# Operands stacked to 128 rows or columns in a recurrent-attention stage, and the powers and sums of its triangular inverse formed together

## The chip, the cores and the metric

One core of one Trainium2 chip runs the whole program. The metric is the device time of one launch in microseconds (us). Work is spread over TensorE (PE; its weight loads are shown apart as PEld), VectorE (DVE), ScalarE (ACT), GpSimd (POOL), and the DMA queue of SyncE (SP).

## What is computed

Two blocks follow each other: a recurrent attention (4 sequences, 8 heads, 768 tokens, head size 40), whose output rows then go through a mixture of 8 experts.

```python
for t in range(S):                       # state: 40x40 per sequence and head
    y[:, :, t] = einsum('bhd,bhde->bhe', r_t, state)
    Sa = einsum('bhde,bhe->bhd', state, a_t)
    state = state * w_t[:, :, None, :] - einsum('bhd,bhe->bhde', Sa, b_t)
    state = state + einsum('bhd,bhe->bhde', v_t, k_t)
x = y rearranged to (3072, 320)
expert = argmax(x @ w_gate); p = softmax weight of that expert
out = p * (relu(x @ w1[expert]) @ w2[expert])
```

## The kernel before

**Units.** The attention is cut into chunks of C = 64 tokens. One unit is one chunk of two sequences with all their heads (16 heads, laid out as NP = 4 pairs by two halves of the 128 partitions, each half holding 40 rows of a head). There are 24 units (12 chunks, two pairs of sequences in turn); a unit needs the state that the unit two before it left. Every product is in f32, and a matmul in f32 shows as two matmul records and two weight-load records in the trace; a transpose shows as one of each.

**What a unit does** (`unit`, L363 to L683). SP loads the decay (`dec`, L387) and one tile `in` with the five operands k, a, b, v, r (L388): four DMAs each. DVE scans the decay into running products (L389, L397), and POOL scales b, a and k by them (L400). Then PE works in steps, and each step's result in PSUM is taken out by DVE or ACT:

- `p_n` (L428): the products of a and b in both orders, 32 matmuls; masked by DVE (L436) they give the strictly triangular matrix N and its transpose, both in `X`.
- The inverse of the triangular matrix, as a product of (1 + N^k) for k = 1, 2, 4, ..., 32 (L440 to L494). `plus_one` on POOL adds the identity (L442); `moved` carries the transposed factor to the other halves (L463, four matmuls with 256 moving columns); `squares` (L474) squares both N^k and its transpose, 32 matmuls, four times, and a last `times` squares one of them, 16 matmuls; `times` (L445) multiplies each new factor on, 16 matmuls, five times, and `new_TT` copies the product out.
- `p_g` (L500): k with a and v with r, 32 matmuls, masked into `G` (L508). `natural` (L405): transposes of v, k and b, four each.
- The recurrent part: `p_r` (L528, 16 matmuls), `p_gv` (L535, 32), `p_u` (L557, 32), `p_uT` (L581, 16), `p_st` (L593, 32: the new state), `p_z` (L615, 16), `p_y` (L625, 32 in two steps), and `p_x` (L647, four matmuls with 128 stationary and 136 moving columns) that turns the output and forms the expert logits. The last part (L642 to L683) stores the rows of x.

Nearly all of these matmuls have 64 contraction rows and 64 stationary columns, and the loops go round `TILES` (L272), the four quarters of the 128x128 array.

**What sets the order.** Nothing runs as written. Every piece is a `Step` (L181) with a rank, an engine, a cost in us and its readers and writers; `in_order` (L201) picks, again and again, the step that can begin first by these costs (then the lowest rank), finds it PSUM banks (8 in all, two for most steps), and issues it. A step marked ANY goes to ACT or DVE, whichever is free first (L236). The order on each engine is fixed by that list; the engines wait for each other by semaphores. A `Ring` (L281) is a set of buffers taken in turn.

**Expert weights.** `w_pool` (L156) holds two sets of weights. `first_weights` (L688) loads the sets of experts 0 and 1 in the middle of the attention; later sets are loaded two experts ahead (L871). After the attention come routing (L696 to L798), then for each expert gather, transposes, layer 1 (L821), layer 2 (L836) and the scattered store.

Of the kernel before, what the change touches and what calls it, by code (L numbers as in the profile page):

```python
# [23 lines left out]
def kernel(  # L24
# [62 lines left out]

    ihalf = consts.tile([128, HP], F32)
    m_nn = consts.tile([128, 2, C], F32)
    m_up = consts.tile([128, C], F32)  # L90
    nc.gpsimd.memset(m_nn[:], -1.0)
    nc.gpsimd.memset(m_up[:], 1.0)
    for h in range(2):
        hs = slice(h * HP, (h + 1) * HP)
        nc.gpsimd.tensor_copy(ihalf[hs], ident[hs, hs])
        nc.gpsimd.affine_select(
            m_nn[hs, 0, :], m_nn[hs, 0, :], compare_op=ALU.is_gt, fill=0.0, base=0, pattern=[[-1, C]], channel_multiplier=1,
        )
        nc.gpsimd.affine_select(
            m_nn[hs, 1, :], m_nn[hs, 1, :], compare_op=ALU.is_gt, fill=0.0, base=0, pattern=[[1, C]], channel_multiplier=-1,  # L100
        )
        nc.gpsimd.affine_select(
            m_up[hs], m_up[hs], compare_op=ALU.is_gt, fill=0.0, base=0, pattern=[[1, C]], channel_multiplier=-1,
        )
# [51 lines left out]
    w_pool = ctx.enter_context(tc.tile_pool(name="moe_w", bufs=2))  # L156

    def fetch(w1, w2):
        t1 = w_pool.tile([128, DB, F], F32, name="w1")
        t2 = w_pool.tile([128, FB, Dm], F32, name="w2")  # L160
# [11 lines left out]
    PE, DVE, ACT, POOL, SP, ANY = "PE", "DVE", "ACT", "POOL", "SP", "ANY"  # L172
    steps = []
# [7 lines left out]
    class Step:  # L181
        def __init__(self, rank, eng, cost, fn, reads=(), writes=(), after=(), lag=0.2):
            self.rank, self.eng, self.cost, self.fn, self.lag = (rank, len(steps)), eng, cost, fn, lag
# [17 lines left out]
    def in_order():  # L201

        free = {e: 0.0 for e in (PE, DVE, ACT, POOL, SP)}
        bank_free = [0.0] * 8

# [25 lines left out]
        while ready:  # L231
# [26 lines left out]
            free[e] = t + cost  # L258
            s.done = t + cost + s.lag
# [16 lines left out]
    with tc.tile_pool(name="ring", bufs=1) as ring, \  # L276
# [18 lines left out]
        r_in = Ring("in", [5, SEG, C], 4, 5)  # L295
# [5 lines left out]
        r_nat = [Ring("nat" + n, [NP, 2, HP], 3) for n in "VKB"]  # L301
        r_X = Ring("X", [2, 2, NP, C], 5, 2)
        r_M = Ring("M", [2, NP, C], 3)
        r_TT = Ring("TT", [2, NP, C], 4)
        r_G = Ring("G", [2, 2, NP, C], 2, 2)
# [3 lines left out]
        r_U = Ring("U", [2, NP, D], 2)  # L309
        r_uT = Ring("uT", [2, NP, C], 2)  # L310
        r_ZT = Ring("ZT", [2, NP, C], 2)
# [10 lines left out]
        for i, (t, held) in enumerate(r_dec.bufs):  # L322
# [5 lines left out]
            Step(-100 + 5 * i, DVE, 1.2, fn, writes=held)  # L328
# [31 lines left out]
        eye = ihalf[:, None, None, :].to_broadcast([128, 2, NP, C])  # L360
        state = {}

        def unit(u):  # L363
            c, bh = divmod(u, BH)
            last = c + 1 == NCH
            I, hI = r_in.take()
            (dec, hdec), (qi, hqi), (rv, hrv), (qq, hq), (pc, hpc) = (r.take() for r in (r_dec, r_qini, r_rv, r_q, r_pc))
            r3 = rv[:, : SEG * C1].rearrange("p (s j) -> p s j", j=C1)
            q3 = qq[:].rearrange("p (s j) -> p s j", j=C1)
            behind = rv[:, 2:].rearrange("p (s j) -> p s j", j=C1)[:, :, :C]  # L370


            at, w0 = divmod(c * C, CW)
            dst = dec[:, : SEG * C1].rearrange("x (p q j) -> x q p j", q=2, j=C1)
            dst5 = I[:].rearrange("x n (p q) j -> x q n p j", q=2)

            def load(e, part):
                for q in range(2):
                    for par in range(2):
                        src = packed[2 * bh + q, at, par, :, :, :, w0 : w0 + C]  # L380
                        if part == 0:
                            nc.sync.dma_start(dst[rows(par), q, :, 1:], src[:, 0])
                        else:
                            nc.sync.dma_start(dst5[rows(par), q], src[:, 1:])
# [15 lines left out]
            for n, by, hb in ((B_, behind, hrv), (A, q3[:, :, :C], hq), (K, behind, hrv)):  # L400
                Step(pre, POOL, 1.22, lambda e, n=n, by=by: nc.gpsimd.tensor_tensor(I[:, n], I[:, n], by, op=ALU.mult),  # L401
                     reads=hb, writes=hI[n : n + 1])


            def natural(rank, r, n):  # L405
                t, hn = r.take()
                ps = Held(1)

                def turned(e):
                    for p in range(NP):  # L410
                        nc.tensor.transpose(  # L411
                            psum[:, ps.at, p * 128 : (p + 1) * 128], I[:, n, 2 * p : 2 * p + 2, :].rearrange("x q t -> x (q t)"),
                            ident[:],
                        )
                Step(rank, PE, 0.55, turned, reads=hI[n : n + 1], writes=[ps])
                Step(rank, ANY, 0.59, lambda e: copy(e, t[:].rearrange("c p a d -> c (p a d)"), psum[:, ps.at, :]),
                     reads=[ps], writes=hn)
                return t, hn

            def head(n, p, q, par):  # L420
                return I[halves[par], n, 2 * p + q, :]

# [5 lines left out]
            def p_n(e, ps=ps):  # L428
                t = whole(ps)
                for p in range(NP):  # L430
                    for w, (l, r) in enumerate(((A, B_), (B_, A))):
                        for par, q in TILES:
                            mm(t[halves[1 - q], par, w, p, :], head(l, p, q, par), head(r, p, q, par))
            Step(u, PE, 8 * ROUND, p_n, reads=[hI[A], hI[B_]], writes=[ps])
            for s in range(2):
                Step(u, DVE, 0.69, lambda e, s=s, ps=ps, X=X: nc.vector.tensor_tensor(  # L436
                    X[:, s], whole(ps)[:, s], m_nn[:, :, None, :].to_broadcast([128, 2, NP, C]), op=ALU.mult,
                ), reads=[ps], writes=hX[s : s + 1])

            def plus_one(x, hx, w):  # L440
                m, hm = r_M.take()
                Step(u, POOL, 1.25, lambda e: nc.gpsimd.tensor_tensor(m[:], x[:, :, w], eye, op=ALU.add), reads=hx, writes=hm)  # L442
                return m, hm

            def times(stat, mov, reads, ps):  # L445

                def fn(e):
                    t = pair(ps, C)
                    for p in range(NP):
                        for h, s in TILES:  # L450
                            mm(t[halves[s], h, p, :], stat(h, s, p), mov(h, s, p))
                Step(u, PE, 4 * ROUND, fn, reads=reads, writes=[ps])

            def new_TT(ps):
                t, ht = r_TT.take()
                Step(u, ANY, 0.59, lambda e: copy(e, t[:], pair(ps, C)), reads=[ps], writes=ht)
                return t, ht


            T1, hT1 = plus_one(X, hX, 1)  # L460
            ps = Held(2)

            def moved(e, ps=ps):  # L463
                t = pair(ps, C)
                for h, s in TILES:
                    mm(t[halves[s], h].rearrange("x p j -> x (p j)"), ihalf[halves[h]], T1[halves[h], s].rearrange("x p j -> x (p j)"))
            Step(u, PE, 4 * ROUND, moved, reads=hT1, writes=[ps])
            TT, hTT = new_TT(ps)
            k = 1
            while 2 * k < C:  # L470
                nk = 2 * k
                ps = Held(2)
                if 2 * nk < C:
                    def squares(e, ps=ps, X=X):  # L474
                        t = whole(ps)
                        for p in range(NP):
                            for w in range(2):
                                for h, s in TILES:
                                    mm(t[halves[s], h, w, p, :], X[halves[h], s, 1 - w, p, :], X[halves[h], s, w, p, :])
                    Step(u, PE, 8 * ROUND, squares, reads=hX, writes=[ps])  # L480
                    X, hX = r_X.take()
                    for s in range(2):
                        Step(u, ANY, 0.59, lambda e, s=s, ps=ps, X=X: copy(e, X[:, s], whole(ps)[:, s]),
                             reads=[ps], writes=hX[s : s + 1])
# [438 lines left out]
```

## Time and profile before

| | us |
|---|---|
| three runs | 1102.62, 1093.54, 1095.27 |
| median of the runs | 1095.27 |
| the profiled execution, its own time | 1102.44 |
| its span, from first to last instruction | 1100.7 |

The profile is of one execution. Its views used below: the page's totals; the waits (who waited for whom, in total us, times, longest); the timeline (instructions of one kind merged: start, length from the first start to the last end, engine, line, operation, tiles, shape, count, and in brackets the idle time before it and what ended it; "issue" means that the engine waited for nothing that the profile shows); the groups by line and shape (busy us, mean ns of one | idle time before); and tables of stretches. Lengths of matmul records overlap each other, so the pace of a run of them is read from one start to the next. The attention runs from about 30 to 719 us, the rest of the span is routing and the experts.

### The profile page before, as it was taken

How to read it: one execution, taken by the hardware profiler on the slowest of the kernel's cores; microseconds unless marked ns; L12 is line 12 of the kernel's file. 1: busy time of each engine (PE TensorE's matmuls, PEld its weight loads, DVE VectorE, ACT ScalarE, POOL GpSimd, SP SyncE). 2: the span in 40 equal slices, each digit the busy share in tenths (PEclk: the TensorE clock that was granted, in tenths of full speed). 3: DMA queues.
4: the chain of work that ended last, by engine and by line, in shares of the span. 5: the costliest groups of instructions: out<-in, count | busy, mean ns of one | idle time of the engine just before them, and what ended most of it. 6: DMA issues, size and time to landing. Idle time of an engine off the chain costs nothing. (4 is left out here: it accounts for less than half of the span.)

```text
span 1100.7 us, 50357 instructions
## 1 busy us (share of the span) xinstructions
PE 837.7 (76%) x23644; PEld 614.6 (56%) x23644; DVE 400.8 (36%) x769; ACT 247.5 (22%) x504; POOL 340.1 (31%) x318
## 2 busy tenths in 40 slices
PE   1676776876676667676777676728999999999996
PEld 1666666765665556666766665612535535535534
DVE  5445444454444434544554444361120110111110
ACT  1233333322223323223322232300101011010000
POOL 9544333343433413433343332125202202101001
PEclk9999899899989979998999899957999999999998
DMA  5222222222220381221222100003322223113000
GB/s 104 49 40 53 46 46 47 43 49 40 44 51 8 76 222 29 46 46 35 57 47 46 34 11 16 11 6 96 94 93 87 90 81 106 60 55 113 12 6 19
DMA packets 112678, 60.95 MB, mean 55 GB/s; under 512 B 96849, under 2 KB 108115, under 8 KB 112468
## 3 DMA queue, kind: packets, MB, share of 16 engines
q1 hardware_dynamic: 109056, 48.51, 19.0%
q0 software_dynamic: 3072, 9.18, 2.9%
q8 instruction: 186, 3.05, 1.2%
q14 instruction: 24, 0.20, 0.1%
q10 hardware_dynamic: 340, 0.01, 0.0%
HBM read 49.82 MB, written 9.18 MB: 54 GB/s over the span
## 5 line engine op out<-in xcount | busy, mean ns | idle before, releaser
L442 POOL TENSOR_TENSOR M<-X,ihalf 128x512 f32<-128x512 f32 x120 | 165.0, 1378 | 349.3 <-DVE X L355 194.0
L358 PE MATMUL ps<-X 64*64 64x64 f32 x6912 | 148.1, 228 | 68.3 <-issue 67.0
L827 PE MATMUL hp<-xgT,w 128*128 128x512 f32 (+1 forms) x384 | 192.2, 630 | 0.0
L358 PEld LDWEIGHTS ps<-X 64*64 64x64 f32 x6912 | 131.1, 142 | 79.2 <-issue 75.7
L840 PE MATMUL zp<-w,h_sb 128*128 128x320 f32 x512 | 145.0, 433 | 0.0
L827 PEld LDWEIGHTS hp<-xgT,w 128*128 128x128 f32 (+1 forms) x384 | 63.4, 190 | 123.4 <-issue 122.3
L358 PE MATMUL ps<-TT,M 64*64 64x64 f32 x3840 | 94.9, 228 | 37.2 <-issue 36.7
L353 ACT COPY TT<-ps 128x512 f32<-128x512 f32 x122 | 71.6, 587 | 193.5 <-PE ps L358 187.0
L840 PEld LDWEIGHTS zp<-w,h_sb 128*128 128x128 f32 x512 | 94.5, 191 | 34.5 <-issue 0.8
L832 DVE TENSOR_SCALAR h_sb<-hp 128x512 f32<-128x512 f32 x32 | 22.1, 692 | 247.5 <-PE hp L827 244.4
L358 PEld LDWEIGHTS ps<-TT,M 64*64 64x64 f32 x3840 | 79.5, 141 | 45.2 <-issue 43.2
L353 ACT COPY X<-ps 128x512 f32<-128x512 f32 x109 | 62.8, 587 | 172.0 <-PE ps L358 170.0
L355 DVE COPY X<-ps 128x512 f32<-128x512 f32 x83 | 57.3, 690 | 107.6 <-PE ps L358 106.2
L846 POOL DMA_INDIRECT out_dram<-zo,s_idx x32 | 31.7, 992 | 181.3 <-ACT zo L845 180.1
L358 PE MATMUL ps<-in 64*64 64x64 f32 x3072 | 61.6, 223 | 23.8 <-issue 23.5
L401 POOL TENSOR_TENSOR in<-in,rv 128x512 f32<-128x512 f32 x48 | 60.8, 1276 | 47.5 <-DMA in<-in_packed_dram 39.6
L411 PE MATMUL ps<-ident,in 128*128 128x128 f32 x288 | 48.8, 309 | 28.6 <-DMA in<-in_packed_dram 21.3
L358 PEld LDWEIGHTS ps<-in 64*64 64x64 f32 x3072 | 54.7, 137 | 27.2 <-issue 26.5
L834 ACT ACTIVATE h_sb<-hp 128x512 f32<-128x512 f32 x32 | 19.1, 597 | 203.1 <-PE hp L827 164.5
L808 POOL DMA_INDIRECT xg<-x_rows,g_idx x32 | 30.8, 963 | 109.0 <-PE tp L818 78.9
L411 PEld LDWEIGHTS ps<-ident,in 128*128 128x128 f32 x288 | 35.0, 155 | 34.0 <-issue 25.2
L845 ACT COPY zo<-zp 128x320 f32<-128x320 f32 x32 | 13.6, 426 | 134.3 <-PE zp L840 134.3
(163 smaller groups left out, 1072.5 us busy)
## 6 DMA issues: line engine op xcount, KB each, us to landing
in<-in_packed_dram SPq DMA_DIRECT2D x96, 200.0 KB
w<-in_moe_w_dram SPq DMA_DIRECT2D x8, 1280.0 KB
w<-in_moe_w_dram SPq DMA_DIRECT2D x8, 1024.0 KB
dec<-in_packed_dram SPq DMA_DIRECT2D x96, 40.0 KB
x_rows<-xs SPq DMA_DIRECT2D x48, 80.0 KB
w<-in_moe_w_dram SPq DMA_DIRECT2D x8, 256.0 KB
xg<-x_rows,g_idx POOLq DMA_INDIRECT x32
out_dram<-zo,s_idx POOLq DMA_INDIRECT x32
```

Source lines behind the costliest of these rows:

```text
L353: nc.scalar.copy(dst, src)
L355: nc.vector.tensor_copy(dst, src)
L358: nc.tensor.matmul(out_, lhsT=lhsT, rhs=rhs, start=start, stop=stop, skip_group_check=True)
L401: Step(pre, POOL, 1.22, lambda e, n=n, by=by: nc.gpsimd.tensor_tensor(I[:, n], I[:, n], by, op=ALU.mult), reads=hb, writes=hI[n : n + 1])
L411: nc.tensor.transpose(psum[:, ps.at, p * 128 : (p + 1) * 128], I[:, n, 2 * p : 2 * p + 2, :].rearrange("x q t -> x (q t)"), ident[:],)
L442: Step(u, POOL, 1.25, lambda e: nc.gpsimd.tensor_tensor(m[:], x[:, :, w], eye, op=ALU.add), reads=hx, writes=hm)
L808: nc.gpsimd.indirect_dma_start(out=g["xg"][:, j, :], out_offset=None, in_=x_d[:, :], in_offset=bass.IndirectOffsetOnAxis(ap=g["gi"](j), ax ...
L827: nc.tensor.matmul(hp[:, :cols], lhsT=g["w"][0][:dsz, db, fb * 128 : (fb + 1) * 128], rhs=g["xT"][:dsz, db, :cols], start=(db == 0), stop= ...
L832: nc.vector.tensor_relu(g["h"][:, fb, :cols], hp[:, :cols])
L834: nc.scalar.activation(g["h"][:, fb, :cols], hp[:, :cols], AF.Relu)
L840: nc.tensor.matmul(zp[:], lhsT=g["h"][:, fb, j * 128 : (j + 1) * 128], rhs=g["w"][1][:, fb, :], start=(fb == 0), stop=(fb == FB - 1),)
L846: ins_ = nc.gpsimd.indirect_dma_start(out=out[:, :], out_offset=bass.IndirectOffsetOnAxis(ap=g["si"](j), axis=0), in_=zo[:], in_offset=Non ...
```

## The change

A unit's operands are laid out anew. k and b of a head lie side by side in one tile `KB`, v and u in `Vu` (v is loaded a second time, alone, into `V2`). So a product that both need is one matmul with 128 stationary columns (`p_ka`, `p_z`), and a sum over both is one matmul with 128 rows (`p_y`, which also forms the new state in the same matmul, as 40 further columns). In the inverse, a power N^k, its transpose and the running sum lie beside each other in `X`, so that one matmul with 128 moving columns gives the next transposed power and the product for the sum; the sum's own old value is added by a product with the identity (`p_sum`) in place of POOL's addition. `p_sq` forms the first squares, `p_move` is `moved` with the identity added by DVE, and `p_last` multiplies the last factor on. The 24 steps' ring buffers change in number. Loads go by operand: seven loads of four DMAs per unit in place of two of four, for the first unit in part from ACT's queue. The planner's steps carry a number of instructions `n`, and its PE clock waits for pages of them. The weights of expert 0 get a pool of their own and are still loaded early; those of expert 1 are loaded behind the attention.

```diff
+    PAGE, FETCH = 256, 3.6
...
+            while left:
+                if not page[0]:
+                    end = max(end, page[1])
+                    page[:] = [PAGE, end + FETCH]
...
-        for i, (t, held) in enumerate(r_in.bufs):
-            for lo in (32, 96):
-                zero(-99 + 5 * i, POOL if lo == 32 else DVE, 1.2, t[lo : lo + 32], held)
+                    for lo in (32, 96):
+                        zero(-99 + 9 * i + j, POOL if lo == 32 else DVE, 0.5, t[lo : lo + 32], held)
...
-            Step(u - 3, SP, 1.7, lambda e: load(e, 0), writes=hdec, lag=2.5)
-            Step(u - 3, SP, 1.7, lambda e: load(e, 1), writes=hI, lag=3.5)
+            other = ACT if u == 0 else SP
+            load(SP, 0, by_q(dec[:, : SEG * C1].rearrange("x (s j) -> x s j", j=C1)[:, :, 1:]), hdec)
+            load(other, 1 + B_, lambda q: KB[:, :, 1 + q, :], hKB)
+            load(SP, 1 + K, lambda q: KB[:, :, 3 * q, :], hKB)
+            load(other, 1 + A, by_q(Aq), hA)
+            load(SP, 1 + V, by_q(V2), hV2)
+            load(other, 1 + R, by_q(R_), hR)
+            load(SP, 1 + V, lambda q: Vu[:, :, 3 * q, :], hV)
...
+            def p_ka(e, ps=ps):
+                for p in range(NP):
+                    for q in range(2):
+                        for par in range(2):
+                            mm(psum[:, ps.at + par, (2 * p + q) * C : (2 * p + q + 1) * C], both(KB, p, q, par), head(Aq, p, q, par))
...
-                Step(u, POOL, 1.25, lambda e: nc.gpsimd.tensor_tensor(m[:], x[:, :, w], eye, op=ALU.add), reads=hx, writes=hm)
...
+            while 4 * k <= C:
+                end = 4 * k == C
+                Step(u, PE, 4 * ROUND, lambda e, ps=ps, X=X: p_power(e, ps, X, 1, 0), reads=hX[: 2 if k == 2 else 3], writes=[ps], n=64)
...
+                w = 1 if end else 2
+                def p_sum(e, ps=ps, X=X, w=w):
+                    for p in range(NP):
+                        for h, s in TILES:
+                            mm(t[halves[s], h, p], X[halves[h], s, p, 0, :], X[halves[h], s, p, 3 - w : 3, :], start=(p == 0), stop=False)
+                    for h, s in TILES:
+                        mm(t[halves[s], h, :, w - 1, :], ihalf[halves[h]], X[halves[h], s, :, 2, :], start=False)
...
+                def p_yr(e):
+                    for p in range(NP):
+                        for q in range(2):
+                            for par in range(2):
+                                mm(y_at()[halves[par], q, p, :C], Sn[halves[par], q, p, :], head(R_, p, q, par), start=(p == 0), stop=False)
...
+            def p_z(e, ps=ps):
+                            mm(psum[:, ps.at + par, (2 * p + q) * C : (2 * p + q + 1) * C], both(Vu, p, q, par), head(R_, p, q, par))
...
+            w = C if last else C + D
+            def p_y(e):
+                            mm(y_at()[halves[par], q, p, :w], nKB[:, 2 * p + q, par, :], ZU[:, par, 2 * p + q, :w],
+                               start=(c == 0 and p == 0))
...
         def first_weights(e):
-            for i in range(2):
-                weights[i] = fetch(moe_w1[i], moe_w2[i])
+            weights[0] = fetch(w_first, moe_w1[0], moe_w2[0])
...
+    w_pool = ctx.enter_context(tc.tile_pool(name="moe_w", bufs=2))
+    weights[1] = fetch(w_pool, moe_w1[1], moe_w2[1])
```

## Rows read from the trace of the kernel before

**Rows 1.** The page: span, PE's totals, and the instruction queue (packets, MB, share).
```profile
span 1100.7 us, 50357 instructions
...
PE 837.7 (76%) x23644; PEld 614.6 (56%) x23644; DVE 400.8 (36%) x769; ACT 247.5 (22%) x504; POOL 340.1 (31%) x318
...
q8 instruction: 186, 3.05, 1.2%
```
**Rows 2.** The waits of PE: total us, times, longest.
```profile
PE ps L358 <- issue: 193.7, 149, 4.5
...
PE ps L358 <- ACT TT L353: 2.4, 6, 0.7
```
**Rows 3.** Timeline of PE, 264.5 to 283 us.
```profile
266.94 0.87 PE L358 MATMUL ps<-X 64*64 64x64 f32 x45 [1.91 <-issue]
...
268.62 0.41 PE L358 MATMUL ps<-X 64*64 64x64 f32 x15
270.61 0.93 PE L358 MATMUL ps<-X 64*64 64x64 f32 x48 [1.58 <-issue]
271.47 1.19 PE L358 MATMUL ps<-turn_gate,xT 128*128 128x136 f32 x8
272.60 0.69 PE L358 MATMUL ps<-TT,M 64*64 64x64 f32 x32
...
274.53 1.05 PE L358 MATMUL ps<-X 64*64 64x64 f32 x57 [0.67 <-issue]
275.40 0.61 PE L358 MATMUL ps<-M,ihalf 64*64 64x256 f32 x8
275.84 0.64 PE L358 MATMUL ps<-TT,M 64*64 64x64 f32 x32
276.33 0.78 PE L358 MATMUL ps<-X 64*64 64x64 f32 x31
278.17 0.73 PE L358 MATMUL ps<-X 64*64 64x64 f32 x33 [1.07 <-issue]
...
281.64 0.27 PE L358 MATMUL ps<-TT,M 64*64 64x64 f32 x1 [1.38 <-issue]
```
**Rows 4.** The whole attention: us, busy (count) by engine, PEclk, DMA share, GB/s.
```profile
30.00:720.00 690.00, 486.87 (x22607) 441.65 (x22605) 322.95 (x574) 210.33 (x432) 245.28 (x186) 0.94 0.23 47
```
**Rows 5.** Timeline of PE: transposes at 338 us, expert layer 2 at 824 us.
```profile
338.07 1.09 PE L411 MATMUL ps<-ident,in 128*128 128x128 f32 x8
339.09 0.62 PE L358 MATMUL ps<-TT,M 64*64 64x64 f32 x25
...
823.62 8.78 PE L840 MATMUL zp<-w,h_sb 128*128 128x320 f32 x32
```
**Rows 6.** Groups by line and shape: weight loads of three shapes.
```profile
L358 PEld LDWEIGHTS ps<-X 64*64 64x64 f32 x6912 | 131.1, 142 | 79.2 <-issue 75.7 <-ACT TT L353 1.9 <-DVE sa L605 0.4
L827 PEld LDWEIGHTS hp<-xgT,w 128*128 128x128 f32 x256 | 44.4, 191 | 74.2 <-issue 73.0
L827 PEld LDWEIGHTS hp<-xgT,w 64*128 64x128 f32 x128 | 19.0, 186 | 49.3 <-issue 49.3
```
**Rows 7.** Timeline of SP and of PE around the first weights, 390 to 406 us.
```profile
390.22 0.59 SPq L162 DMA_DIRECT2D w<-in_moe_w_dram  x1
...
401.43 0.48 PE L358 MATMUL ps<-TT,rhs 64*64 64x64 f32 x5 [4.55 <-issue]
```
**Rows 8.** Timeline of SP: issues of one load of four DMAs.
```profile
90.48 3.59 SPq L384 DMA_DIRECT2D in<-in_packed_dram  x4
97.18 2.50 SPq L382 DMA_DIRECT2D dec<-in_packed_dram  x4
```
**Rows 9.** Timeline of PE: the attention's first and last product, the experts' first.
```profile
30.37 2.97 PE L358 MATMUL ps<-in 64*64 64x64 f32 x128
...
717.38 2.18 PE L358 MATMUL ps<-turn_gate,xT 128*128 128x136 f32 x8 [0.79 <-DVE xT L637]
...
750.71 1.92 PE L827 MATMUL hp<-xgT,w 128*128 128x512 f32 x2
```

More of the change, by code (lines that the diff above doesn't have):

```diff
@@ L204, in in_order @@
         bank_free = [0.0] * 8
+        page = [0, 0.0]
         opened = set()
@@ L257, in in_order @@
                 bank_free[b : b + h.banks] = [None] * h.banks
-            free[e] = t + cost
-            s.done = t + cost + s.lag
+            end = t
+            left = s.n
+            while left:
+                if not page[0]:
+                    end = max(end, page[1])
+                    page[:] = [PAGE, end + FETCH]
+                k = min(left, page[0])
+                page[0] -= k
+                left -= k
+                end += cost * k / s.n
+            if not s.n:
+                end += cost
+            free[e] = end
+            s.done = end + s.lag
             s.fn(e)
@@ L399, in unit @@
             ), reads=hdec + hqi, writes=hq)
[L400 to L418, printed above, removed]
@@ L420, in head @@
-            def head(n, p, q, par):
-                return I[halves[par], n, 2 * p + q, :]
+            for i in range(2):
+                ps_ = slice(2 * i, 2 * i + 2)
+                kb = KB[:, ps_].rearrange("x p (q s) j -> x (p q) s j", s=2)
+                by = behind[:, 4 * i : 4 * i + 4].unsqueeze(2).to_broadcast([128, 4, 2, C])
+                Step(pre, POOL, 1.25, lambda e, kb=kb, by=by: nc.gpsimd.tensor_tensor(kb, kb, by, op=ALU.mult),
+                     reads=hrv, writes=hKB[i : i + 1])
@@ new lines, in unit, with p_n @@
+            up = m_up[:, None, :, :].to_broadcast([128, NP, 2, C])
+            for s in range(2):
+                Step(u, DVE, 0.69, lambda e, s=s, ps=ps: nc.vector.tensor_tensor(
+                    GA[:, s], psum[:, ps.at + s, :].rearrange("x (p q j) -> x p q j", p=NP, q=2), up, op=ALU.mult,
+                ), reads=[ps], writes=hGA[s : s + 1])
+            X1, hX1 = r_N.take()
+            ps = Held(2)
+            def p_n(e, ps=ps):
+                t = pair(ps, C)
+                for p in range(NP):
+                    for par, q in TILES:
+                        mm(t[halves[1 - q], par, p, :], head(Aq, p, q, par), KB[halves[par], p, 1 + q, :])
@@ L429, in p_n @@
                 t = whole(ps)
                 for p in range(NP):
[L431 to L438, printed above, removed]
@@ new lines, in unit, with p_move @@
+            Step(u, PE, 8 * ROUND, p_sq, reads=hX1 + hGA, writes=[ps], n=128)
+            for h in range(2):
+                Step(u, ANY, 0.59, lambda e, h=h, ps=ps, X=X: copy(
+                    e, X[:, h, :, 0:2, :].rearrange("x p w j -> x w p j"), whole(ps)[:, h],
+                ), reads=[ps], writes=hX[h : h + 1])
+            ps = Held(2)
+            def p_move(e, ps=ps):
+                t = pair(ps, C)
+                for h, s in TILES:
+                    mm(t[halves[s], h], ihalf[halves[h]], GA[halves[h], s, :, 1 - h, :])
@@ new lines, in unit, with p_power @@
+            Step(u, PE, 4 * ROUND, p_move, reads=hGA, writes=[ps], n=16)
+            Step(u, DVE, 0.69, lambda e, ps=ps, X=X: nc.vector.tensor_tensor(X[:, :, :, 2, :], pair(ps, C), eye(2, NP), op=ALU.add),
+                 reads=[ps], writes=hX[2:3])
+            def p_power(e, ps, X, l, r):
+                t = pair(ps, C)
+                for p in range(NP):
+                    for h, s in TILES:
+                        mm(t[halves[s], h, p, :], X[halves[h], s, p, l, :], X[halves[h], s, p, r, :])
@@ L461, in unit, with p_last @@
+                k *= 2
+            TF, hTF = r_TF.take()
             ps = Held(2)
-            def moved(e, ps=ps):
+            def p_last(e, ps=ps):
                 t = pair(ps, C)
[L465 to L484, printed above, removed]
-                    M, hM = plus_one(X, hX, 0)
-                else:
-                    times(lambda h, s, p, X=X: X[halves[h], s, 1, p, :], lambda h, s, p, X=X: X[halves[h], s, 0, p, :], hX, ps)
-                    M, hM = r_M.take()
-                    Step(u, DVE, 0.69, lambda e, ps=ps, M=M: nc.vector.tensor_tensor(M[:], pair(ps, C), eye, op=ALU.add),
-                         reads=[ps], writes=hM)
-                ps = Held(2)
-                times(lambda h, s, p, M=M: M[halves[h], s, p, :], lambda h, s, p, TT=TT: TT[halves[h], s, p, :], hM + hTT, ps)
-                TT, hTT = new_TT(ps)
-                k = nk
@@ L511, in unit @@
-            nV, hnV = natural(u, r_nat[0], V)
-            nK, hnK = natural(u, r_nat[1], K)
-            nB, hnB = natural(u, r_nat[2], B_)
+                for p in range(NP):
+                    for h, s in TILES:
+                        mm(t[halves[s], h, p, :], M[halves[h], s, p, :], TT[halves[h], s, p, :])
+            Step(u, PE, 4 * ROUND, p_last, reads=hM + hTT, writes=[ps], n=64)
+            Step(u, ANY, 0.59, lambda e, ps=ps: copy(e, TF[:], pair(ps, C)), reads=[ps], writes=hTF)
+            nV, hnV = r_nV.take()
@@ new lines, in unit @@
+            ZU, hZU = r_ZU.take()
+            ps = Held(2)
+            def p_z(e, ps=ps):
+                for p in range(NP):
+                    for q in range(2):
+                        for par in range(2):
+                            mm(psum[:, ps.at + par, (2 * p + q) * C : (2 * p + q + 1) * C], both(Vu, p, q, par), head(R_, p, q, par))
+            Step(u, PE, 1.71, p_z, reads=hV + huT + hR, writes=[ps], after=before_z, n=64)
+            for s in range(2):
+                Step(u, DVE, 0.69, lambda e, s=s, ps=ps: nc.vector.tensor_tensor(
+                    ZU[:, s].rearrange("x (p q) j -> x p q j", q=2)[:, :, :, :C],
+                    psum[:, ps.at + s, :].rearrange("x (p q j) -> x p q j", p=NP, q=2),
+                    m_plus[:, None, None, :].to_broadcast([128, NP, 2, C]), op=ALU.mult,
+                ), reads=[ps], writes=hZU[s : s + 1])
@@ L603, in unit @@
+            w = C if last else C + D
+            def p_y(e):
+                for p in range(NP):
+                    for q in range(2):
+                        for par in range(2):
+                            mm(y_at()[halves[par], q, p, :w], nKB[:, 2 * p + q, par, :], ZU[:, par, 2 * p + q, :w],
+                               start=(c == 0 and p == 0))
+            Step(u, PE, 8 * 2 * w / 2400, p_y, reads=hnKB + (hZU[:2] if last else hZU), writes=[psy], n=64)
+            if not last:
                 sa2, hsa2 = r_sa[bh].take()
@@ L625, in p_y @@
-            def p_y(e, w, stat, mov):
-                t = pair(psy, C)
-                for p in range(NP):
-                    for q, par in TILES:
-                        mm(t[halves[par], q, p, :], stat[halves[q], p, par, :], mov(p, q, par),
-                           start=(c == 0 and w == 0 and p == 0), stop=(w == 1))
-            Step(u, PE, 4 * ROUND, lambda e: p_y(e, 0, nB, lambda p, q, par: ZT[halves[q], par, p, :]),
-                 reads=hnB + hZT, writes=[psy])
-            Step(u, PE, 4 * ROUND, lambda e: p_y(e, 1, nK, lambda p, q, par: G[halves[q], par, 1, p, :]),
-                 reads=hnK + hG, writes=[psy])
```

265 lines of the change are left out of this document (145 added, 120 removed).

## The prediction

> **What bounds the kernel now.** First the page's totals [rows 1]: PE is busy for 76% of the span, no other engine for more than 36%. That alone doesn't say what bounds the attention, so next the waits of PE [rows 2]: 193.7 us of PE's idle time, in 149 pieces, end in "issue", and the largest wait for another engine's result inside the attention products is 2.4 us in all. In the attention PE waits for nobody's data and yet stands still. The timeline [rows 3] shows the pattern: PE runs fast, stops, and goes on at 266.94, 270.61, 274.53, 278.17 and 281.64 us, every 3.47 to 3.92 us. Between the stops lies the same number of records: from 274.53 to 278.17 it is 57 + 8 + 32 + 31 = 128. A matmul record has a weight-load record beside it, so that is 256 instructions. The page's instruction queue [rows 1] moved 186 packets; 23,644 x 2 PE instructions over 186 is 254 each. I read it so: PE gets its instructions in blocks of 256, fetched one at a time, and a block that is worked off in less than about 3.8 us is followed by a stop until the next one is there. The last group before the stop at 270.61 begins at 268.62 and is 0.41 us long, of which one record is 0.23: the 128 records of that block were issued in 268.80 - 266.94 = 1.86 us, half of the 3.67 us that the block took.
>
> The whole stage agrees. It runs from 30.4 us to the end of the last product at 719.6 [rows 9], 689 us or 28.7 per unit. By the loops, a full unit has 472 matmuls (two records each) and 12 transposes (one each), 956 records or 7.47 blocks; 28.7 / 7.47 is 3.84 us per block, and I use this as the price of a block. DVE, ACT and POOL are busy for 323, 210 and 245 of 690 us [rows 4] and follow.
>
> **What the change does to the blocks.** Matmuls per full unit after: p_ka 16, p_n 16, p_sq 32, p_move 4, four powers 64, four sums 80, p_last 16, p_r 16, p_gv 32, p_uT 16, p_yr 16, p_z 16, p_y 16, p_x 4: 344, with 4 + 8 + 8 = 20 transposes. That is 708 records, 5.53 blocks, 21.2 us at 3.84. If fetching stays the bound, a unit falls from 28.7 to 21.2 us.
>
> **What it does to PE's own work**, which now comes into view. The steps, with the time from one start to the next:
> - 64x64 matmuls round the four quarters (p_n, p_sq, powers, p_last, p_r, p_gv, p_uT): 384 records at 1.86 us / 128 = 14.5 ns [rows 3]: 5.6 us.
> - p_move: 8 records with 256 columns. Before, 275.40 to 275.84: 0.44 us for 8 [rows 3].
> - Sums: 128 moving columns aren't in the trace; between 14.5 ns (64 columns) and 55 ns (256), on the line, 28 ns. Three sums of 32 such records and 8 with 256 columns: 3 x (0.90 + 0.44); the last has 64 columns: 0.46 + 0.44. Together 4.9 us. Were 128 columns as quick as 64 or as slow as 256, 1.3 less or 2.6 more.
> - p_yr goes round two quarters only, so 32 records cost 0.46 to 0.93; I take 0.93.
> - Transposes: a group of eight takes 339.09 - 338.07 = 1.02 us [rows 5], and p_x 272.60 - 271.47 = 1.13 [rows 3]. Going over from quarters to the whole array costs something before it: 48 records from 270.61 end their issue at 271.31, p_x begins at 271.47, 0.16 later. So 1.18 twice, 0.7 for the group of four, 1.29 for p_x: 4.35 us.
> - p_ka and p_z (64 rows, 128 columns, 64 moving): not in the trace. Below, 32 records at 14.5 ns, 0.46 us; above, one after another like transposes, 32 x 1.02/8 = 4.1 us. Two such products, on the upper and the lower rows, should run side by side: half of the upper end, 2.05 each, 4.1 us.
> - p_y (128 rows, 64 columns, 104 moving): layer 2 of the experts moves 320 columns in 8.78 / 32 = 0.27 us per record [rows 5], 0.84 ns per column, so 87 ns for 104, two side by side: 32 x 43 ns, and 0.3, an estimate from p_x, for going over and back: 1.7 us, between 0.46 and 4.1.
>
> The sum is 22.0 us. The same list for the kernel before (928 records, p_move, three groups of four transposes, p_x) gives 13.5 + 0.4 + 2.2 + 1.3 = 17.4, while PE was busy for 487 us in the stage [rows 4]; less 149 stops, into each of which 0.23 us of the last record reaches, that is 453 / 24 = 18.9 us. The list misses 8%. With it, a unit after is 23.8 us of PE work, above the 21.2 of fetching. So PE's own work becomes the bound, and fetching adds to it where a block is light.
>
> How much it adds depends on how light and heavy steps fall into blocks. Evenly mixed, nothing: 23.8 us. Wholly apart, the 768 light instructions are three blocks at 3.84 = 11.5 us in place of 6.0, a unit 29.3. A block holds two to six steps of different kinds, so I stand nearer to mixed, a quarter of the way: 25.2 us. 24 units are 605 us, 84 less than now.
>
> [...]
>
> **The rest, part by part.**
> - DVE and ACT: PSUM results of 512 columns are 25 per unit before and 25 after, by the steps; those of 320 are six and seven. 533 / 24 = 22 us on two engines in a unit of 25 [rows 4]: off the path as a sum, though each hand-over is on it (a rival below). POOL loses five additions per unit and is no bound.
> - SP: 28 load issues per unit in place of eight. Four issues of 40 KB took 2.50 us, four of 200 KB 3.59 [rows 8]; seven groups at 2.50 are 17.5 us and stores some 1, below 25, with units loaded three ahead. Nothing added, but cover is thin: behind a late store seven loads queue. The bounds are 0 and, if SP's order stalls the loads by 2 us per unit, 48 us. Nearest is the row, so 0.
> - Weights: while two sets are loaded, PE stops for 4.55 us after "issue" [rows 7], some 3 over the usual, and its neighbours add about as much. One set halves it, -4 us. The second set comes behind the attention, beneath the 31 us of routing up to the first expert product at 750.7 [rows 9] and beneath expert 0; if it delays the first gather, up to +5. I take -4 in all.
> - Start: zeroing, scaling and first loads have about the same bytes; the first product came at 30.4 us [rows 9]. Between -5 and +3; I take 0. Routing and experts keep their code.
>
> Sum: 1102.44 - 84 - 4 = 1014. The profiled execution lies 7.2 above the median of the runs, so 1007 us against 1095.27. A measurement of this kernel tells about 1% from no change.
>
> **Rivals.**
> - *Fetching stays the bound* (28%): the wide products are cheaper than taken, or mixing is perfect. 24 units at 21.4 us are 514: 1102 - 175 - 4 - 7 = 916 at the best; halfway to the forecast, 960. For it: nothing in the trace shows 64 x 128 products as slow as I take them. Against: transposes do cost 128 ns each. [...]
> - *Hand-overs become the bound* (17%): now PE never waits for data because it is always late. With some 20 PE steps per unit, each waiting 0.1 us more for DVE or ACT, a unit gains 2 us: 27.2, 653 us, and 1055. For it: the new chain sum, copy, next power is strictly serial. Against: several units are in work at once.
> - *Slower than before* (7%): the wide products don't run side by side. p_ka, p_z and p_y at 4.1 us each add 6.5 x 1.08 = 7 us per unit: 32.2, 773 us, and 1175. It decides from 28.7 us per unit, 3.5 above the forecast, when the 96 wide records cost about 95 ns on average in place of 60. For it: a load of 128 columns takes 186 ns on 64 rows and 191 on 128, against 142 for 64 columns [rows 6], so half the rows save nothing in a load.
> - *It doesn't do what it says* (3%): the stops aren't tied to the count of instructions, and the stage stays near 28.7 us per unit, about 1095.
>
> **How the numbers follow.** The forecast has 45%, 980 to 1040. The range reaches into the first rival and to the hand-overs: 930 to 1070. Below 1% faster lie the forecast, the first two rivals but for their edges: 0.88. Around no change the last rival and late hand-overs: 0.05. Slower: 0.07.
>
> **What would show it.** PE records 17,804 (24 x 708 less what the first and last units lack, and 1,020 of the experts); instruction packets near 140; "issue" of PE well below 100 us, and stops still 128 records apart where they stand. p_ka's 32 records in about 2 us, p_y's in 1.7, a sum's 40 in 1.34. Waits of PE for DVE and ACT should appear, some 20 us. I am wrong if stops of 128 records still fill the stage (first rival), if PE's waits for DVE and ACT exceed 60 us (second), or if p_ka takes over 3.5 us (third).

## The result and the profile after

| | us |
|---|---|
| four runs after, median | 998.91 (993.15 to 1006.34) |
| four runs before beside them, median | 1098.94 (1093.54 to 1102.69) |
| ratio, with its 95% interval | 0.910 (0.902 to 0.918) |
| the profiled execution after, its span | 994.6 |
| forecast | 1007, 930 to 1070 |

The changed kernel is 9% faster. The page of its profile, beside [rows 1]: PE has 17,804 records and the instruction queue 140 packets, both as counted from the loops, and PE is now busy for 90% of the span.

```profile
span 994.6 us, 39246 instructions
...
PE 895.2 (90%) x17804; PEld 651.6 (66%) x17804; DVE 393.3 (40%) x801; ACT 250.3 (25%) x508; POOL 172.9 (17%) x206
...
q8 instruction: 140, 2.29, 1.0%
```

The waits of PE after, beside [rows 2]: "issue" has fallen from 193.7 us in 149 pieces to 8.3 in 17, and DVE and ACT are now among those that PE waits for.

```profile
PE ps L571 <- DMA V<-in_packed_dram: 22.7, 1, 22.7
...
PE ps L385 <- issue: 8.3, 17, 1.1
...
PE ps L385 <- DVE M L529: 6.2, 3, 2.8
PE ps L385 <- DVE ZU L666: 4.8, 5, 2.4
PE ps L385 <- ACT TF L380: 3.8, 14, 0.7
PE ps L385 <- DVE S L382: 3.8, 3, 2.0
```

The 22.7 us is the wait for the first operands at the start. The timeline of PE after, 249 to 285 us, is to be held against [rows 3]: the regular stops are gone, and the wide products can be read off.

```profile
256.12 0.61 PE L385 MATMUL ps<-X,ihalf 64*64 64x256 f32 x8
256.55 1.10 PE L385 MATMUL ps<-R,S 64*64 64x64 f32 x32
257.58 2.00 PE L385 MATMUL ps<-A,KB 64*128 64x64 f32 x32
259.51 1.57 PE L385 MATMUL ps<-X 64*64 64x64 f32 x64
...
269.92 2.00 PE L385 MATMUL ps<-R,Vu 64*128 64x64 f32 x32 [0.33 <-ACT Vu L644]
271.85 1.10 PE L580 MATMUL ps<-ident,Vu 128*128 128x128 f32 x8
...
273.99 1.65 PE L385 MATMUL ps<-ZU,nKB 128*64 128x104 f32 x32
275.56 1.10 PE L385 MATMUL ps<-X 64*64 64x128 f32 x32
276.49 0.61 PE L385 MATMUL ps<-X,ihalf 64*64 64x256 f32 x8
276.92 0.20 PE L385 MATMUL ps<-ihalf,ST 64*64 64x40 f32 x2
...
281.91 2.00 PE L385 MATMUL ps<-A,KB 64*128 64x64 f32 x32
```

From one p_ka to the next it is 281.91 - 257.58 = 24.3 us: one unit. From start to start p_ka takes 1.93 us, p_z 1.93, p_y 1.57, the 32 records of a sum with 128 columns 0.93 and its 8 with the identity 0.43. The prediction had 2.05, 2.05, 1.7, 0.90 and 0.44. The attention begins and ends as follows, to be held against [rows 9].

```profile
28.16 3.68 PE L385 MATMUL ps<-A,KB 64*128 64x64 f32 x32
...
611.83 2.18 PE L385 MATMUL ps<-turn_gate,xT 128*128 128x136 f32 x8 [0.78 <-DVE xT L699]
```

From the first start to the last end that is 586 us against 689, so the stage lost 103 us, the start 2, and the 381 us behind the stage are the same in both. The stretch view of nearly the whole stage shows who is busy: PE 534 of 570 us, DVE 311, ACT 213, POOL 80.

```profile
30.00:600.00 570.00, 534.30 (x16610) 470.30 (x16608) 311.18 (x584) 212.57 (x435) 80.33 (x69) 0.99 0.25 56
```

One count from the trace makes the kernels below comparable. Between neighbouring starts of PE's records and weight loads, every gap over 0.25 us is a stop; a stop that ends 1.0 to 1.75 us after an instruction packet landed is put down to fetching (in the kernel before nearly all are, 9.8 of 10.3 us per unit), the others are taken for hand-overs (waits for another engine's result). What remains is PE's own work, with shorter waits in it. All in us per unit, from one profiled execution each; the whole stage of one kernel varies by some 1% between executions. The last column is the time, in us for the whole stage, at the lower of the two levels of the granted clock.

| kernel | stage | stops, fetch | stops, other | rest | packets | half clock |
|---|---|---|---|---|---|---|
| before | 28.7 | 9.8 | 0.5 | 18.4 | 186 | 78 |
| after | 24.4 | 0.9 | 2.3 | 21.2 | 140 | 26 |
| before_repeat | 30.3 | 10.5 | 0.6 | 19.2 | 198 | 64 |
| before_inverse | 26.1 | 6.4 | 0.8 | 18.9 | 174 | 10 |
| before_dveplus | 28.2 | 9.0 | 0.9 | 18.4 | 186 | 65 |
| before_weights | 28.2 | 9.2 | 0.5 | 18.4 | 186 | 72 |
| after_repeat | 26.1 | 1.6 | 2.1 | 22.4 | 152 | 43 |
| after_quarters | 23.9 | 2.0 | 2.6 | 19.3 | 152 | 27 |
| after_onehalf | 28.4 | 0.8 | 2.3 | 25.3 | 140 | 122 |
| after_dvesum | 23.7 | 0.8 | 2.6 | 20.3 | 134 | 45 |
| after_both | 23.7 | 2.6 | 2.6 | 18.4 | 146 | 40 |
| after_blind | 24.2 | 0.7 | 2.3 | 21.3 | 140 | 26 |
| after_dvesum_blind | 22.6 | 0.6 | 1.8 | 20.2 | 134 | 22 |
| after_dvesum_costs | 23.9 | 0.8 | 2.7 | 20.4 | 134 | 48 |

So fetching gave back 8.9 us per unit, PE's own work grew by 2.8, other stops by 1.8: 4.3 net. Two cautions. A stop falls into the window for fetching by chance too: with the landing times shifted by 2 to 20 us, 0.5 us per unit of the changed kernel's stops still fall into it, so about half of its 0.9 may not be fetching. And the column of other stops names no cause: of the changed kernel's 55 us there (2.3 in 24 units), the waits of PE in the stage put 22.4 us down to DVE and 8.0 to ACT.

The granted clock has two levels in these traces, full speed and half of it (1.00 and 0.50). The kernel before ran its stage at the lower one for 78 us, in 18 pieces (0.94 on the mean [rows 4]), the changed kernel for 26 us in four; its clock records begin at 35.4 us. The longest piece inside the attention before, from 401.0 us, came behind the stop of 4.55 us [rows 7]; the pieces at 291.4 and 506.5 us in the changed kernel came behind stops of 2.1 and 2.4 us. The stretch view and the timeline of PE before:

```profile
401.10:414.60 13.50, 10.84 (x316) 9.65 (x320) 3.67 (x7) 1.76 (x3) 1.27 (x1) 0.50 1.00 248
...
404.62 1.11 PE L358 MATMUL ps<-in,uT 64*64 64x64 f32 x32
405.50 1.08 PE L358 MATMUL ps<-M,ihalf 64*64 64x256 f32 x8
406.36 0.65 PE L358 MATMUL ps<-X 64*64 64x64 f32 x14
```

Here 32 records of 64x64 take 0.88 us from start to start, where 0.46 is usual, and eight with 256 columns 0.86 in place of 0.44 [rows 3]. An estimate from this: with the intervals in such pieces put at the pace of the others, PE's own work is 17.1 us per unit before, 18.7 in before_inverse and 20.8 after. The clock is no rival to fetching as the bound before: 128 such records at 27 ns are 3.5 us, still under the price of a block. Of the 103 us it accounts for some 22 at most.

### The profile page after: what moved, and what is told of

It is laid out like the page before. It is cut to its first block, busy times and chain, and to the rows that moved or that the text cites. A ratio compares the mean times of both kernels' runs of the same rounds, so it can differ in the third digit from the quotient of the medians.

```text
span 994.6 us, 39246 instructions
## 1 busy us (share of the span) xinstructions
PE 895.2 (90%) x17804; PEld 651.6 (66%) x17804; DVE 393.3 (40%) x801; ACT 250.3 (25%) x508; POOL 172.9 (17%) x206
## 5 line engine op out<-in xcount | busy, mean ns | idle before, releaser
L385 PE MATMUL ps<-X 64*64 64x64 f32 (+1 forms) x6144 | 151.4, 243 | 6.9 <-issue 3.5
L380 ACT COPY X<-ps 128x512 f32<-128x512 f32 x175 | 99.9, 586 | 122.8 <-PE ps L385 116.6
L451 POOL TENSOR_TENSOR KB<-KB,rv 128x512 f32<-128x512 f32 x48 | 56.6, 1200 | 209.4 <-DMA KB<-in_packed_dram 85.2
L453 POOL TENSOR_TENSOR A<-A,q 128x512 f32<-128x512 f32 x24 | 28.4, 1183 | 231.6 <-PE ps L385 121.7
L385 PE MATMUL ps<-X,ihalf 64*64 64x256 f32 x768 | 60.6, 377 | 1.1 <-issue 1.1
L436 DVE TENSOR_TENSOR_SCAN rv<-dec,ones 128x521 f32<-128x521 f32 x24 | 29.8, 1244 | 59.2 <-DMA dec<-in_packed_dram 57.7
L385 PE MATMUL ps<-R,Vu 64*128 64x64 f32 x768 | 50.9, 284 | 1.7 <-ACT Vu L644 1.6
L385 PE MATMUL ps<-A,KB 64*128 64x64 f32 x768 | 51.1, 286 | 0.0
L385 PEld LDWEIGHTS ps<-R,Vu 64*128 64x128 f32 x768 | 47.4, 196 | 5.0 <-ACT Vu L644 2.1
L385 PEld LDWEIGHTS ps<-A,KB 64*128 64x128 f32 x768 | 47.7, 198 | 2.3 <-POOL A L453 0.4
L467 DVE TENSOR_TENSOR GA<-ps,m_up 128x512 f32<-128x512 f32 x48 | 31.2, 685 | 39.2 <-PE ps L385 39.1
```

What stands on the lines that cost most here:

```text
L380: nc.scalar.copy(dst, src)
L385: nc.tensor.matmul(out_, lhsT=lhsT, rhs=rhs, start=start, stop=stop, skip_group_check=True)
L436: Step(pre, DVE, 1.4, lambda e: nc.vector.tensor_tensor_scan(rv[:, : SEG * C1 + 1][:, ::-1], dec[:, ::-1], ones65[:, ::-1], 0.0, op0=ALU.m ...
L451: Step(pre, POOL, 1.25, lambda e, kb=kb, by=by: nc.gpsimd.tensor_tensor(kb, kb, by, op=ALU.mult), reads=hrv, writes=hKB[i : i + 1])
L453: Step(pre, POOL, 1.22, lambda e: nc.gpsimd.tensor_tensor(Aq[:], Aq[:], q3[:, :, :C], op=ALU.mult), reads=hq, writes=hA)
L467: Step(u, DVE, 0.69, lambda e, s=s, ps=ps: nc.vector.tensor_tensor(GA[:, s], psum[:, ps.at + s, :].rearrange("x (p q j) -> x p q j", p=NP, ...
```

## The experiments

Ratios are to the kernel before, run beside each on the same chip; the changed kernel stands at 0.910.

**before_repeat and after_repeat: the same 32 matmuls more per unit.** In both kernels:

```diff
 def p_uT(e, ps=ps):
-    for p in range(NP):
+    for p in [p for p in range(NP) for _ in range(3)]:
```

> The kernel before with every matmul of p_uT issued three times: 32 more matmuls, 128 more PE instructions per unit, 0.93 us of PE work per unit at 14.5 ns a record. Block theory (PE's instructions come in blocks of 256 and a block takes at least 3.84 us): half a block more per unit, 1.92 us, +46 us in all, some 1145. Rival, PE's own work is the bound: at most +22 us. Rival, the hand-overs to POOL, DVE and ACT are the bound and PE has slack: about 0.

Measured: 1138.39 us, ratio 1.043 (1.035 to 1.051), +47 us. PE's own work rose by 0.8 us per unit, the time by 1.6 to 2. The number of stops went up with the packets, 186 to 198, as this row of PE's waits shows beside [rows 2]:

```profile
PE ps L358 <- issue: 212.7, 159, 4.1
```

Twelve packets more and ten stops more: before the change, the price of an instruction was its share of a block, 47 us / 12 = 3.9 us per block, not its work. PE's own work was not the bound, nor did PE have slack.

> The same addition to the changed kernel. If PE's own work is now the bound, as forecast: +22 us, up to +30 with some blocks too light. Rival, fetching still bounds it: +46 us. Rival, hand-overs bound it: well under +22.

Measured: ratio 0.947 (0.939 to 0.954), 0.037 above the changed kernel, +40 us. With both intervals that is 28 to 52: more than 22, at the upper end of the 22 to 30 or beyond it, and 46 for fetching lies inside as well. By the table PE's own work rose by 1.2 us per unit, in part by more time at the half clock (43 us in place of 26), and the stops for blocks by 0.7. The 48 matmuls of p_uT now stand in one run of 192 quick instructions, so the block that holds them is too light: the bound is PE's work only on the whole, and inside a unit a run of quick matmuls still pays by the block. That reading fits the table; no run spreads the same matmuls out.

**after_quarters: the wide products cut back.** For p_ka, and p_z likewise (`cols` stands for the slice of columns):

```diff
-for par in range(2):
-    mm(psum[:, ps.at + par, cols], both(KB, p, q, par), head(Aq, p, q, par))
+for par, s in TILES:
+    mm(psum[halves[s], ps.at + par, cols], KB[halves[par], p, 2 * q + s, :], head(Aq, p, q, par))
```

> The changed kernel with p_ka and p_z cut back into 64x64 quarters: 32 matmuls each in place of 16, so 128 more instructions per unit, but 2.2 us less PE work per unit (0.93 us each in place of 2.05). Block theory: blocks 6.03 per unit, 23.2 us at 3.84, against 20 us of work; a unit stays about where it is, within 12 us of the changed kernel. Rival, only PE's work counts now: -53 us. Rival, fetching still is the bound: +46 us.

Measured: ratio 0.907 (0.902 to 0.913): no difference from the changed kernel that can be told. PE's own work fell by 1.9 us per unit (2.2 expected), 1.1 came back as stops for blocks and some 0.35 as others. For these two products stacking gains nothing: together they save half a block and pay with nearly as much PE time.

**after_onehalf: no neighbour on the other rows.** For p_ka, and p_z likewise:

```diff
-for p in range(NP):
-    for q in range(2):
-        for par in range(2):
+for par in range(2):
+    for p in range(NP):
+        for q in range(2):
```

> The changed kernel with the loops of p_ka and p_z turned, so that first all eight products on the upper 64 rows are issued and then all eight on the lower: the same matmuls and instructions, but no product has a neighbour on the other rows. If the measured 2.05 us come from two products side by side, as the prediction chose: 4.1 us each, 2 x 2.05 x 24 = +98 us, less what the hand-overs and the blocks hide now, +70 to +98. Rival, a product with 128 columns costs its 64 ns a record on either half and nothing runs side by side: 0.

Measured: 1086.6 us, ratio 0.984 (0.980 to 0.988), 0.0745 above the changed kernel: +82 us. The timeline of PE shows p_ka at 3.31 us from start to start, 103 ns a record, in place of 1.93:

```profile
241.01 3.39 PE L385 MATMUL ps<-A,KB 64*128 64x64 f32 x32
244.32 1.16 PE L385 MATMUL ps<-X 64*64 64x64 f32 x64
```

This piece ran at the full clock (1.00 from 240 to 250 us). For p_ka and p_z the step that the third rival of the prediction hung on is settled: products on the upper and the lower rows overlap when they are issued in turn, and an order of the loops that keeps them apart gives back most of the gain of the change, 82 of 99 us. Whether the products or their weight loads overlap, the run doesn't tell. The two products account for 2 x 1.38 us in 24 units, 66 us; the stage also stood at the half clock for 122 us in place of 26, which can be the other 16 but isn't tested apart.

**after_dvesum: the sums without the identity.**

```diff
-mm(t[halves[s], h, p], X[halves[h], s, p, 0, :], X[halves[h], s, p, 3 - w : 3, :], start=(p == 0), stop=False)
-for h, s in TILES:
-    mm(t[halves[s], h, :, w - 1, :], ihalf[halves[h]], X[halves[h], s, :, 2, :], start=False)
+mm(t[halves[s], h, p], X[halves[h], s, p, 0, :], X[halves[h], s, p, 3 - w : 3, :])
...
+Step(u, ANY, 0.59, lambda e, ps=ps, Xn=Xn: copy(e, Xn[:, :, :, 1, :], two_of(ps)[:, :, :, 0, :]), reads=[ps], writes=hXn[0:1])
+Step(u, DVE, 0.69, lambda e, ps=ps, Xn=Xn, X=X: nc.vector.tensor_tensor(
+    Xn[:, :, :, 2, :], two_of(ps)[:, :, :, 1, :], X[:, :, :, 2, :], op=ALU.add), reads=[ps] + hX, writes=hXn[1:2])
```

> The changed kernel without the products with the identity in p_sum; the old sum is added by DVE while it takes the product out of PSUM (the powers are copied apart). 64 instructions and 1.87 us of PE work less per unit, the evacuations as many but more of them on DVE. Block theory with PE's work as the bound: -30 to -45 us. Rival, hand-overs are the bound now: no gain or a loss, DVE having more to do.

Measured: 977.37 us, ratio 0.898 (0.893 to 0.903), 0.0115 below: -13 us. A gain (2 to 23 us with both intervals), but less than the 30 to 45 expected. PE's rest fell by 0.9 us per unit in place of 1.87, and the other stops rose from 2.3 to 2.6. In the rest of the changed kernel the products with the identity make up 1.4 us, not 1.87; where the remaining 0.5 went isn't shown (waits shorter than the 0.25 us of the count sit in the rest). What the edit added is seen in the waits of PE: those for DVE in the stage rose from 22.4 us in 19 pieces to 34.3 in 36, the new addition (L550) among them:

```profile
PE ps L385 <- DVE X L550: 7.9, 9, 2.0
```

**before_inverse: one part alone.** The kernel before with the changed inverse (p_sq, p_move, p_power, p_sum, p_last) on the old layout:

```diff
-                    M, hM = plus_one(X, hX, 0)
...
+                        mm(t[halves[s], h], ihalf[halves[h]], N_[halves[h], s, 1, :, :])
...
+                        mm(t[halves[s], h, :, w - 1, :], ihalf[halves[h]], X[halves[h], s, :, 2, :], start=False)
...
+            weights[0] = fetch(w_first, moe_w1[0], moe_w2[0])
```

> One part alone: the kernel before with the inverse of the changed kernel (powers and sums together, identity products, no additions on POOL), and for space in SBUF the second set of expert weights behind the attention as in the change. k, b, v, u are not stacked. 128 instructions less and some 1.6 us more PE work per unit. Block theory: 6.97 blocks at 3.84 us are 26.8 us per unit, -35 to -46 us. Rival, the gain of the change came from POOL's additions leaving the chain of hand-overs: about the whole of it, near -100 us. Rival, PE's own work bounded the kernel before: +38 us.

Measured: 1040.33 us, ratio 0.951 (0.944 to 0.958): -54 us. Half a block less per unit took 12 packets away; at 3.84 us these are 46. The rest may be noise or the moved weights (below). PE's own work at the full clock is 1.6 us per unit more by the estimate above, as expected, and cost nothing that can be seen. The step from 0.951 to 0.910, 45 us for 34 packets and not the 131 of 34 blocks, is left to the stacking of operands with its loads, buffers, planner and the move of expert 0's weights; no run has the stacking alone, and by after_quarters p_ka and p_z have no part in it that can be told. There PE's own work took over.

**before_dveplus: the additions off POOL.**

```diff
-Step(u, POOL, 1.25, lambda e: nc.gpsimd.tensor_tensor(m[:], x[:, :, w], eye, op=ALU.add), reads=hx, writes=hm)
+Step(u, DVE, 0.69, lambda e: nc.vector.tensor_tensor(m[:], x[:, :, w], eye, op=ALU.add), reads=hx, writes=hm)
```

> The kernel before with the five additions of the identity per unit on DVE (0.69 us each) in place of POOL (1.38 us). PE's instructions are the same in number. Block theory: no change, within 8 us. Rival, hand-overs through POOL were the bound: -30 us or more.

Measured: ratio 0.998 (0.996 to 1.001). Nearly halving the time of five hand-overs per unit (1.38 us on POOL, 0.76 on DVE in the two traces) changed nothing: the chain through POOL was hidden.

**before_weights: the second set of weights behind the attention.**

```diff
-            for i in range(2):
-                weights[i] = fetch(moe_w1[i], moe_w2[i])
+            weights[0] = fetch(w_first, moe_w1[0], moe_w2[0])
...
+    weights[1] = fetch(w_pool, moe_w1[1], moe_w2[1])
```

> The kernel before with one change alone: the weights of expert 1 are loaded behind the attention, not in it. By the prediction's term: -4 us (0.4%); the stretch of slow blocks around the load is half as long. Rival, the second load then delays the first gather: +5 us or no gain.

Measured: ratio 0.998 (0.995 to 1.001). Inconclusive: -4 us lies in the interval, and so does 0. The records tell more. From 2 us ahead of the first load's issue to 30 us behind it, PE of the kernel before issued 772 records, where 32 us of the rest of its stage have 1,063: some 9 us lost to two sets. In this run it issued 1,009 against 1,073: 2 us lost to one set. And the changed kernel goes further than this run: its set of expert 0 is issued at the very start, so that, unlike in [rows 7], no set is loaded within the attention. Its timeline of SP:

```profile
0.80 0.44 SPq L166 DMA_DIRECT2D w<-in_moe_w_dram  x1
...
618.65 0.41 SPq L166 DMA_DIRECT2D w<-in_moe_w_dram  x1
```

**after_both, after_blind, after_dvesum_blind, after_dvesum_costs: combinations and the planner.** after_both joins the edits of after_quarters and after_dvesum. The other three change the order alone, against the changed kernel or against after_dvesum:

```diff
-    PAGE, FETCH = 256, 3.6
+    PAGE, FETCH = 256, 0.0
```

and for the costs

```diff
-    ROUND = 0.116
+    ROUND = 0.133
...
-            Step(u, PE, 1.71, p_ka, reads=hKB + hA, writes=[ps], n=64)
+            Step(u, PE, 2.05, p_ka, reads=hKB + hA, writes=[ps], n=64)
...
-            Step(u, PE, 8 * 2 * w / 2400, p_y, reads=hnKB + (hZU[:2] if last else hZU), writes=[psy], n=64)
+            Step(u, PE, 16 * 2 * w / 2400, p_y, reads=hnKB + (hZU[:2] if last else hZU), writes=[psy], n=64)
```

> The changed kernel with p_ka and p_z in quarters and the sums added by DVE: 64 more instructions, 4.1 us less PE work per unit. Block theory: 5.78 blocks, 22.2 us per unit at the least, against 18 us of work: a unit 22.2 to 23.3 us, -26 to -50 us against the changed kernel. Rival, only PE's work counts: -98 us. Rival, hand-overs: no gain.

Measured: ratio 0.896 (0.890 to 0.902), 0.014 below the changed kernel, -15 us, about what after_dvesum gave alone. PE's own work is back at the 18.4 us of the kernel before; fetching takes 2.6 and other stops 2.6. Of the 2.8 us of work taken away 2.1 are given back, most of it to fetching, as the row of PE's waits shows beside the changed kernel's 8.3:

```profile
PE ps L385 <- issue: 41.5, 48, 2.3
```

> The changed kernel with the planner's fetch time set to 0, so that it orders the steps as if instructions were always there; the program is the same but for order and buffers. If the fall in instructions is what brought the gain: 0 to +25 us against the changed kernel. Rival, the gain came from the order: +50 us or more.

Measured: ratio 0.902 (0.896 to 0.909). Not slower; 8 us faster at the middle, but the intervals overlap, so no difference is shown: the gain of the change didn't come from an order that knows of the blocks.

> The sums by DVE and the planner's fetch time at 0, the two edits that each gained about 1%. If what is left is waits that the order decides, they add: about 0.89 of the kernel before. If both remove the same waits: 0.898, as the sums by DVE alone.

Measured: 952.76 us, ratio 0.869 (0.865 to 0.873), more than both gains together: 4% below the changed kernel, and the fastest of the study. PE's work is the same as in after_dvesum (20.2 and 20.3 us per unit); the other stops fell from 2.6 to 1.8 and the fetch stops from 0.8 to 0.6. So it was waits that the new order of the same steps took away: those for DVE in the stage fell from 34.3 us in 36 pieces to 14.1 in 17, and the row for the addition itself from 7.9 us to this:

```profile
PE ps L385 <- DVE X L550: 1.1, 3, 0.4
```

The share of the work that after_dvesum didn't save is not saved here either.

> The sums by DVE, and the planner given the measured costs of PE's steps: p_ka and p_z 2.05 us in place of 1.71, p_y twice its figure, a round of four 0.133 in place of 0.116, the transposes 1.05. If the short waits of PE for DVE and ACT come from an order made for a faster PE: -10 to -20 us against the sums by DVE alone. If they come from the chain itself: 0.

Measured: ratio 0.899 (0.895 to 0.902): nothing. The measured costs of PE's steps didn't bring the order that the simpler planner found; which property of that order does it stays open.

## Why the prediction was right, and where its terms were off

- *The bound before.* Right. The stops of 128 records were fetching: none of the 186 instruction packets of the kernel before begins until the one ahead of it has landed, and from one start to the next it is 3.77 us by the median; before_repeat paid 3.9 us per packet more, before_inverse gained by the packet, and before_dveplus and its shorter hand-overs gained nothing.
- *The blocks after.* 17,804 records as counted, and 140 packets, forecast as near 140.
- *PE's own work.* The list came to 22.0 us per unit and the rest measured 21.2. The 8% put on top, taken from the kernel before, was the mis-sized term: it made 23.8. By the estimate at the full clock the list was close for both kernels (17.4 against 17.1 before, 22.0 against 20.8 after). What it missed before was mostly time at the half clock, 1.3 us per unit, and only 0.4 of that was left after; the prediction put the granted clock of 0.94 in [rows 4] to no use. Of the untested costs, side by side was the right choice for p_ka and p_z (after_onehalf), p_y and the sums were within 0.13 us of their values, and p_yr on its two quarters took 1.03 us, where 0.93 was chosen from 0.46 to 0.93.
- *Blocks that are too light.* 1.4 us per unit forecast, 0.9 measured, of which chance may be half. The share of a quarter was a guess about the order. after_repeat suggests that quick instructions in a row still cost more than their work, 40 us where the work of 64 records is 22.
- *Hand-overs.* Put at nothing in the sum, though some 20 us of waits for DVE and ACT were named as a sign; 2.3 us per unit of other stops measured, 30 us of waits in the stage put down to DVE and ACT. The second rival's 2 us per unit was there in size, but smaller than the over-estimate of PE's work; the two errors, 2.6 too much and 2.3 too little, nearly cancel. That 25.2 us per unit met 24.4 is partly luck.
- *Changes of shape.* The list has 0.16 us for going over from quarters to the whole array, read at one place: 48 records from 270.61 end their issue 0.16 us before p_x [rows 3]. In the trace before, from 30 to 600 us, a record on the whole array starts 0.149 us behind the quarter record ahead of it, by the median of 59 such changes, where quarter records follow each other at 14.5 ns. No run here took such changes away alone, so what they cost in time is not shown.
- *Weights and start.* The term of -4 us took one set to stay in the attention. None does, since expert 0's set is loaded ahead of it; an estimate from the count of records under before_weights puts the term nearer -9 us. The time of before_weights itself can't be told from no change. The start gave 2 us, forecast at 0 with bounds that held it. SP's loads, of thin cover, held: after the start no wait of PE for a load is among its largest.
- *A slip.* The first rival's best case was worked out with 21.4 us per unit, where the blocks give 21.2. That moves its 916 us by 5 and no chance.

## What to carry to other kernels

When stops of an engine stand a fixed count of instructions apart, count the instructions of each form before its flops: in the kernel before an instruction cost its share of a block, 3.9 us per 256 (before_repeat), and half a block less per unit by wider matmuls brought 54 us, of which 12 packets at 3.84 us are 46 (before_inverse). In the changed kernel, where PE's own work of 21.2 us per unit is as long as 5.53 blocks at 3.84 us, 1.9 us of work less for half a block more gained nothing that can be told (after_quarters). Try matmuls on half of the rows in an order of issue that alternates between the halves: for p_ka and p_z it was worth 82 us, with 60 ns a record in place of 103 (after_onehalf). A correction that is taken from the kernel before holds only while its cause does: look at the granted clock first. And once the large bound is gone, try a second order of the same steps: with the sums on DVE it was worth 3%, in the changed kernel itself nothing that can be told.

## What was not expected of the hardware

With 128 stationary columns on 64 rows, records issued in turn to the upper and the lower rows take 60 ns each (p_ka after, 1.93 us for 32), and 103 ns when all on one half come first (after_onehalf, 3.31 us for 32), both at the full clock: the same work costs 1.7 times as much by the order of two loops. And quick matmuls added to a kernel that is bound by its own PE work on the whole cost 40 us (28 to 52, after_repeat), where 64 records at 14.5 ns in 24 units are 22: PE's own work rose by 1.2 us per unit and the stops for blocks by 0.7.
